# Retention and channel mix in one kernel: blocks 3 to 5 in chunks of 64 tokens, more k buffers, and a new written order

## The chip, the core and the metric

One core of a Trainium2 chip runs the whole program. The metric is the device time of one execution in microseconds (us); lower is better. The figures for the kernel before are three runs and one profiled execution, which the hardware profiler took on that core.

## The reference

Two layers follow each other. The first is a recurrent retention over 768 tokens, for 4 batches and 8 heads of 64:

```
state = gamma[h] * state + outer(k[t], v[t])        # 64 x 64 for each head
y[t]  = 0.125 * q[t] @ state
```

The heads of a token are laid side by side, x (4, 768, 512), and a channel mix follows, in which `x_prev` is x shifted by one token:

```
xk = mu_k * x + (1 - mu_k) * x_prev                 # xr the same with mu_r
out = sigmoid(xr @ w_r) * (relu(xk @ w_k) ** 2 @ w_v)   # w_k 512 x 1024, w_v 1024 x 512, w_r 512 x 512
```

All inputs and the output are float32 in HBM.

## The kernel before

**Blocks.** The 768 tokens of each batch are three blocks of 256, so there are twelve blocks, n = 0 to 11; block n belongs to batch n // 3. The recurrence is computed in chunks: inside a chunk the scores of all pairs of tokens (k against q) are masked to the causal half and multiplied with v, and what came before the chunk enters through a carried state. The products with `w_k`, `w_r` and `w_v` follow for each block; blocks 3 and 4, 6 and 7, and 9 and 10 share one set of mixed inputs (`GROUPS`), so that their key products are 512 tokens wide. All products are in float16 and add up in float32 in PSUM, which has eight banks.

**Three forms of the attention part.** A block takes one of three forms, picked by the lists `HALF` and `WIDE`.

| form | blocks before | chunks | scores (`S`) | masks (`M`) | state updates (`U`) | values (`Y`) and reads of the carried state (`I`, `J`) |
|---|---|---|---|---|---|---|
| in neither list ("plain") | 0, 1 | 2 of 128 | 2 words of 16 products, 64x128 (line 393); block 0 in quarters | two 128x1024; block 0 four 128x512 | 2 | `Y` 32 of 64x128 (line 552) with the second read in it, `I` 8 |
| `WIDE` | 2, 3, 4, 5 | 2 of 128 | 2 words of 8 products, 64x128 (line 385) | two 128x1024 | 2 | `Y` 16 of 128x128 (line 541); `I` 8 and `J` 8 (line 504) |
| `HALF` | 6 to 11 | 4 of 64 | one word of 32 products, 64x64 (line 372) | one 128x1024 | 4 | `Y` 32 of 64x64 (line 525) and 16 of line 504; `I` 16 |

The last block of a batch has one state update fewer, the first block of a batch has fewer reads. In the `HALF` form the result of a block (`D`, line 570) is two VectorE operations of 128x512, in the others one of 128x1024 (line 577).

**Turning q and k.** Both have to stand with the head's 64 elements on the partitions. Blocks 3 to 5 do this with eight full 128x128 products for a head pair each (`PAIRQ`, `PAIRK`, line 308), blocks 6 to 8 with 32 products of 64x64 (line 303), blocks 0 to 2 with 16 of 128x64 (line 314), and blocks 9 to 11 with a DMA transpose on SyncE's queue (`DT`, line 348). ScalarE copies what TensorE turned out of PSUM (line 262).

**Order.** Nothing is scheduled: the string `ORDER` is read word by word, and each word appends its instructions to the engines it uses, so the order of the words is the order on each engine and on each queue. A word is `code.block.part@banks~engine`; `v`, `a`, `p`, `s` are VectorE, ScalarE, GpSimd and SyncE. The codes used below:

| code | what | engine |
|---|---|---|
| `lq`, `lk`, `lv` | loads of a block; POOL's queue except the first half of block 0's q and k, which go through SyncE's queue into a staging tile and are cast by ScalarE (`cq`, `ck`) | DMA |
| `wk.0`, `wk.1`, `wr`, `wv.0`, `wv.1` | loads of weights, POOL's queue | DMA |
| `mu` | four small loads of mu_k and mu_r (line 743); `mt`, `me` turn them and copy them out | DMA |
| `z` | filler products of zeros (lines 758, 765): `z.n` is n//4 in float32 and n%4 in float16 | TensorE |
| `Tq`, `Tk`; `Eq`, `Ek` | turn q, k by TensorE; copy out | TensorE; ScalarE |
| `tq`, `tk` | DMA transposes | SyncE's queue |
| `vs` | v times its decay (line 277) | VectorE |
| `S`, `M` | scores, masks (line 417) | TensorE, VectorE |
| `C`, `U`, `G` | state products; updates (line 482, the first of a batch a copy, lines 262 or 264); decay into the next block | TensorE, VectorE or ScalarE |
| `I`, `Y`, `J` | read of the carried state, values, second read | TensorE |
| `D`, `dx` | the block's result x; its difference to the token before (line 592) | VectorE |
| `X.n.0.j`, `X.n.1.j` | mixed inputs xk, xr of head pair j (line 618) | VectorE |
| `K`, `Qa`, `Qb` | keys (lines 632 and 642), relu, square | TensorE, ScalarE, ScalarE |
| `R`, `s` | gate products (line 672), sigmoid | TensorE, ScalarE |
| `V`, `Vc`, `O`, `st` | values of the channel mix (lines 684, 702), result, store | TensorE, VectorE, SyncE's queue |

**Buffers.** q, k and v stand in rings of four tiles (`RING`), the scaled v and the turned q and k in rings of three, and x in one float32 tile for each of three batches (`xT`, batch b in tile b % (B - 1)). A load into a ring waits for the last reader of the tile that it replaces, and every later load on POOL's queue waits with it.

Of the kernel before, what the change touches and what calls it, by code (L numbers as in the profile page):

```python
# [9 lines left out]
F16 = mybir.dt.float16  # L10
F32 = mybir.dt.float32
# [71 lines left out]
def kernel(  # L83
# [543 lines left out]
    def keys(e, n, g, u=None):  # L627
        t0, t1 = part(u)
        k, m = place[n]
        if joint(n):  # L630
            for co in range(NCO):
                nc.tensor.matmul(  # L632
                    banks("K", n, g), lhsT=wk16[:, co, g * P : g * P + P], rhs=XM[0](k)[:, co, :],
                    start=(co == 0), stop=(co == NCO - 1),
                )
            return
        w = 2 if u is None else 4
        pz = banks("K", n, g, *(() if u is None else (u,))).rearrange("p (i t) -> p i t", i=w)
        for i in range(w):
            fo = w * g + i  # L640
            for co in range(NCO):
                nc.tensor.matmul(  # L642
                    pz[:, i, :], lhsT=wk16[:, co, fo * P : fo * P + P],
                    rhs=XM[0](k)[:, co, m * TM + t0 : m * TM + t1],
                    start=(i == 0 and co == 0), stop=(co == NCO - 1), skip_group_check=True,
                )

# [91 lines left out]
    def load_mu(e):  # L739
        for w, x in enumerate((moe_mu_k, moe_mu_r)):  # L740
            y = x.rearrange("(x r c) -> x r c", x=2, c=D)
            for hp in range(2):
                nc.scalar.dma_start(
                    out=mu8[w * NCO : (w + 1) * NCO, low(hp)], in_=y[:, 1:3] if hp else y[:, 0:4:3]
                )

# [48 lines left out]
    def load_wv(e, h):  # L795
# [8 lines left out]
        "D": yout, "dx": differ, "ax": keep, "X": mixed, "K": keys, "Qa": relued, "Qb": squared, "R": gate,  # L804
# [5 lines left out]
    for word in ORDER.split():  # L810
# [4 lines left out]
        if at:  # L815
# [5 lines left out]
            elif code == "V":  # L821
                key = ("V",) + args[:2]
            BANK[key] = [int(x) for x in at]
        CODES[code](ENG.get(eng), *args)


# [28 lines left out]
```

## Time and profile before

| | |
|---|---|
| three runs | 154.51, 155.25, 155.70 us (median 155.25) |
| the profiled execution | 155.54 us; its span, first to last instruction, 153.7 us, so 1.8 us lie around the span |
| granted TensorE clock | 0.997 |
| busy | TensorE 147.1 us, VectorE 128.1, ScalarE 94.4, GpSimd 62.1 (it issues loads) |
| weight products of 512 columns (lines 684, 672, 632) | 376 |
| weight products of 256 columns (lines 642, 702) | 208 |

A matmul's duration in a listing (380 ns for 512 columns) is longer than the step from one matmul to the next, since they overlap. The chain of waits, which gives each stretch of time once, shows the step: 16 such products in a row take 3.45 us there. In the page, PE is TensorE, PEld its weight loads, DVE VectorE, ACT ScalarE, POOL GpSimd and SP SyncE; an engine with a q behind its name is the engine's queue.

### The profile page before, as it was taken

What the parts mean: (1) busy time and instruction counts of PE and PEld (TensorE: products, weight loads), DVE (VectorE), ACT (ScalarE), POOL (GpSimd) and SP (SyncE); (2) the same over time, 40 slices, a digit from 0 to 9 for tenths busy, and PEclk for the clock granted to TensorE, in tenths of its full rate; (3) what the DMA queues carried; (4) which work ended last, traced back from release to release, by engine and by line L of the source; (5) the groups of instructions that cost most, each with busy time, mean ns of one, the idle gap of its engine ahead of it and who ended that gap; (6) DMA issues with size and microseconds to landing.
All of it is one profiled execution on the core that took longest, in us unless ns stands there. A gap on an engine that the chain in (4) does not pass through costs nothing.

```text
span 153.7 us, 4956 instructions
## 1 busy us (share of the span) xinstructions
PE 147.1 (96%) x2129; PEld 82.7 (54%) x2129; DVE 128.1 (83%) x204; ACT 94.4 (61%) x172; POOL 62.1 (40%) x77
## 2 busy tenths in 40 slices
PE   7799899999999999999999999999999999999991
PEld 3245567657864546445448545446664444466450
DVE  1379999999989999999999996999999999421551
ACT  3474339979864689965518817867541089739430
POOL 7974579977967600499979000000000000000000
PEclk9999999999999999999999999999999999999998
DMA  5999999999999995089999999919103013003153
GB/s 138 264 234 194 182 237 235 157 196 203 194 188 203 249 226 194 11 236 156 255 178 249 219 156 161 183 62 106 35 4 141 0 70 141 0 0 136 68 205 136
DMA packets 56525, 23.83 MB, mean 155 GB/s; under 512 B 48056, under 2 KB 52024, under 8 KB 56504
## 3 DMA queue, kind: packets, MB, share of 16 engines
q0 software_dynamic: 45200, 14.95, 80.5%
q1 hardware_dynamic: 10848, 8.26, 21.9%
q10 hardware_dynamic: 456, 0.32, 0.8%
q8 instruction: 16, 0.26, 0.8%
q14 instruction: 5, 0.04, 0.1%
HBM read 24.31 MB, written 6.29 MB: 199 GB/s over the span
## 4 chain that ended last, share of the span: by engine, by line
PE 70%; DVE 14%; DMA 6%; ACT 4%; issue 2%; ACTq 2%; DVEq 0%
PE ps L684 24%; PE ps L672 12%; PE ps L632 10%; PE ps L642 9%; DMA kT<-k 6%; DVE a L417 3%; DVE xk L618 3%; DVE dx L592 2%; DVE vs L277 2%; PE ps L504 2%; PE ps L765 2%; DVE xT L577 2%; PE ps L308 2%; PE ps L372 1%; PE ps L303 1%
## 5 line engine op out<-in xcount | busy, mean ns | idle before, releaser
L684 PE MATMUL ps<-wv,k2s 128*128 128x512 f16 x184 | 43.9, 380 | 0.2 <-ACT kr L651 0.2
L651 ACT ACTIVATE kr<-ps 128x512 f32<-128x512 f32 x48 | 27.8, 594 | 23.4 <-PE ps L632 14.9
L684 PEld LDWEIGHTS <-k2s 128*128 128x128 f16 x184 | 17.3, 98 | 19.1
L690 DVE SCALAR_TENSOR_TENSOR os<-ps,rs 128x512 f32<-128x512 f32 x23 | 15.1, 683 | 12.9 <-PE ps L684 6.5
L672 PE MATMUL ps<-wr,xr 128*128 128x512 f16 x96 | 24.0, 380 | 0.0
L642 PE MATMUL ps<-xk,wk 128*128 128x256 f16 x192 | 23.6, 273 | 0.1
L256 POOL DMA_DIRECT2D v<-in_v_dram x20 | 18.0, 917 | 13.8 <-DVE vs L277 10.9
L632 PE MATMUL ps<-xk,wk 128*128 128x512 f16 x96 | 22.8, 380 | 0.0
L417 DVE TENSOR_TENSOR a<-ps,c_sb 128x1024 f16<-128x1024 f32 (+1 forms) x20 | 21.8, 1109 | 0.8 <-PE ps L393 0.8
L678 ACT ACTIVATE rs<-ps 128x512 f32<-128x512 f32 x24 | 14.3, 594 | 11.4 <-PE ps L672 8.8
L642 PEld LDWEIGHTS <-wk 128*128 128x128 f16 x192 | 18.1, 98 | 4.4 <-DVE xk L618 0.5
L618 DVE SCALAR_TENSOR_TENSOR xr<-dx,mu,xT 128x256 f16<-128x256 f32 (+1 forms) x36 | 19.3, 564 | 0.0
L618 DVE SCALAR_TENSOR_TENSOR xk<-dx,mu,xT 128x256 f16<-128x256 f32 (+1 forms) x36 | 18.9, 567 | 0.3
L256 POOL DMA_DIRECT2D k<-in_k_dram x20 | 17.8, 916 | 2.6 <-DMA wv<-in_moe_w_v_dram 1.2
L277 DVE TENSOR_TENSOR vs<-v,csm_sb 128x1024 f16<-128x1024 f32 x12 | 14.5, 1214 | 2.7 <-DMA v<-in_v_dram 2.7
L659 ACT ACTIVATE k2s<-kr 128x512 f16<-128x512 f32 x24 | 14.7, 626 | 0.4
L592 DVE TENSOR_TENSOR dx<-xT 128x1024 f32<-128x1024 f32 x12 | 14.6, 1219 | 0.2
L663 ACT ACTIVATE k2s<-kr 128x512 f16<-128x512 f32 x24 | 14.5, 626 | 0.3
L632 PEld LDWEIGHTS <-wk 128*128 128x128 f16 x96 | 9.0, 98 | 10.5 <-issue 0.2
L672 PEld LDWEIGHTS <-xr 128*128 128x128 f16 x96 | 9.0, 98 | 10.0
L262 ACT COPY qT<-ps 128x1024 f16<-128x1024 f16 (+1 forms) x10 | 9.2, 925 | 7.5 <-PE ps L314 3.4
L262 ACT COPY kT<-ps 128x1024 f16<-128x1024 f16 (+1 forms) x10 | 9.3, 934 | 7.1 <-PE ps L303 3.4
(73 smaller groups left out, 153.2 us busy)
## 6 DMA issues: line engine op xcount, KB each, us to landing
out_dram<-os SPq DMA_DIRECT2D x23, 256.0 KB, 3.9
v<-in_v_dram POOLq DMA_DIRECT2D x20, 256.0 KB, 6.3
k<-in_k_dram POOLq DMA_DIRECT2D x21, 128.0 KB, 7.1
q<-in_q_dram POOLq DMA_DIRECT2D x13, 128.0 KB, 7.4
q<-in_q_dram POOLq DMA_DIRECT2D x5, 256.0 KB, 8.1
v<-in_v_dram POOLq DMA_DIRECT2D x2, 512.0 KB, 6.9
wv<-in_moe_w_v_dram POOLq DMA_DIRECT2D x2, 512.0 KB, 7.6
wk<-in_moe_w_k_dram POOLq DMA_DIRECT2D x2, 256.0 KB, 9.6
```

The costliest lines, as they stand in the source:

```text
L256: e.dma_start(out=to[:, i, hs], in_=src[:, i])
L262: e.copy(out=out, in_=in_)
L277: e.tensor_tensor(out=VS(n), in0=V32(n).rearrange("p (h i d) -> p i h d", i=2, h=H), in1=gks[:, int(half(n) or wide(n)), :, :, None].to_br ...
L417: nc.vector.tensor_tensor(out=dst, in0=dst if n in SPLITM else src, in1=mask[:, None, None, :].to_broadcast(list(dst.shape)), op=ALU.mult,)
L592: e.tensor_tensor(out=DX(k)[:, :, m * TM + t0 : m * TM + t1], in0=x[:, :, c + t0 : c + t1], in1=x[:, :, c - 1 + t0 : c - 1 + t1], op=ALU.s ...
L618: nc.vector.scalar_tensor_tensor(out=XM[w](k)[:, j, t0:t1], in0=DX(k)[:, j, t0:t1], scalar=mu[:, w * NCO + j : w * NCO + j + 1], in1=x[:, ...
L632: nc.tensor.matmul(banks("K", n, g), lhsT=wk16[:, co, g * P : g * P + P], rhs=XM[0](k)[:, co, :], start=(co == 0), stop=(co == NCO - 1),)
L642: nc.tensor.matmul(pz[:, i, :], lhsT=wk16[:, co, fo * P : fo * P + P], rhs=XM[0](k)[:, co, m * TM + t0 : m * TM + t1], start=(i == 0 and c ...
L651: nc.scalar.activation(out=kr, in_=banks("K", n, g, *u), func=AF.Relu)
L672: nc.tensor.matmul(banks("R", n, tb), lhsT=XM[1](k)[:, co, t : t + P], rhs=wr16[:, co, :], start=(co == 0), stop=(co == NCO - 1),)
L684: nc.tensor.matmul(banks("V", n, tb), lhsT=K2(n)[:, fo, tb * P : tb * P + P], rhs=wv16[:, fo, :], start=(fo == 0), stop=(fo == NFO - 1),)
L690: nc.vector.scalar_tensor_tensor(out=OS(2 * n + tb), in0=banks("V", n, tb), scalar=1.0 / (KSC * KSC), in1=RS(2 * n + tb), op0=ALU.mult, op ...
```

## The change

Blocks 3, 4 and 5 move from the `WIDE` form to the `HALF` form, still turned by the eight head-pair products. `WIDE` is empty: block 2 becomes plain, its loads included (one DMA in place of two for each of k and v). q and v rings grow from four to five tiles, k's to six, and x has two tiles instead of three. The four loads of mu go through SyncE's queue instead of ScalarE's. A variant of the key products (`keys_by_row`, code `Kp`) is added, which no word of the new order uses.

```diff
-HALF = (6, 7, 8, 9, 10, 11)
+HALF = (3, 4, 5, 6, 7, 8, 9, 10, 11)
-WIDE = (2, 3, 4, 5)
+WIDE = ()
-RING = 4
+RING = 5
+RINGK = 6
+XR = 2
+KP = ()
...
-    K16 = ring("k16_", RING, [H * 2 * D], F16)
+    K16 = ring("k16_", RINGK, [H * 2 * D], F16)
...
-    xT = [const.tile([P, NJ, COLS], F32, name=f"xT{b}") for b in range(B - 1)]
+    xT = [const.tile([P, NJ, COLS], F32, name=f"xT{b}") for b in range(XR)]
...
-        return xT[b % (B - 1)], 1 + bi * TM
+        return xT[b % XR], 1 + bi * TM
...
-                nc.scalar.dma_start(
+                (e or nc.scalar).dma_start(
                     out=mu8[w * NCO : (w + 1) * NCO, low(hp)], in_=y[:, 1:3] if hp else y[:, 0:4:3]
                 )
```

The whole order is written anew. Its beginning and its end, before and after:

```diff
-gy.0 lq.0.0.2~s mu lk.0.0.2~s cq.0.0.2~a lv.0~p z.8@7 Tq.0.0.2@0 ck.0.0.2~a vs.0~v Eq.0.0.2~a
-z.3@1 Tk.0.0.2@1 Ek.0.0.2~a z.3@2 S.0.0.0.2@23 lk.0.2.4~p S.0.1.0.2@45 M.0.1.0.2~v Tk.0.2.4@1
-gy.1~a Ek.0.2.4~a lq.0.2.4~p C.0@67 Tq.0.2.4@0 Eq.0.2.4~a U.0.0~v lv.1~p lk.1~p M.0.0.0.2~v
-U.0.1 z.3@4 S.0.1.2.4@45 M.0.1.2.4~v I.0@01 mt@2 me lq.1~p S.0.0.2.4@67 M.0.0.2.4~v lq.2~p G.0~a
-vs.1~v z.4@3 Y.0 Tk.1@6 Ek.1~a D.0~v dx.0~v z.3@3 Tq.1@7 X.0.0.0 Eq.1~a X.0.1.1 wk.1~p C.1@23
-U.1.0 lk.2~p z.4@4 S.1.1@45 M.1.1~v z.1@0 I.1@01 wk.0~p S.1.0@67 M.1.0~v X.0.0.3 Tq.2@4 Eq.2~a
-z.2@5 Y.1 lv.2~p X.0.0.1 X.0.0.2 z.1@5 K.0.2@4 Tk.2@5 D.1~v X.0.1.0 dx.1~v Qa.0.2 X.0.1.2
-X.1.0.0 Ek.2~a K.0.3@0 Qa.0.3 Qb.0.3 X.1.0.2 X.1.0.1 S.2.1@67 K.0.0@5 Qa.0.0 K.0.1@0 X.1.0.3
-K.1.2@1 K.1.0@5 Qb.0.0 wr~p X.1.1.0 Qa.0.1 U.1.1 G.1~a vs.2~v X.0.1.3 Qa.1.0 Qa.1.2 Qb.0.1
...
+lq.0.0.2~s cq.0.0.2~a lv.0~p lk.0.2.4~p gy.0 z.9@7 Tq.0.0.2@0 lq.0.2.4~p vs.0~v Eq.0.0.2~a
+lv.1~p lk.0.0.2~s ck.0.0.2~a z.5@1 Tk.0.0.2@1 Ek.0.0.2~a z.3@2 S.0.0.0.2@23 M.0.0.0.2~v
+S.0.1.0.2@45 M.0.1.0.2~v Tk.0.2.4@1 Ek.0.2.4~a lq.1~p lk.1~p lk.2~p C.0@67 U.0.0~a Tq.0.2.4@0
+Eq.0.2.4~a lq.2~p U.0.1 z.3@1 S.0.1.2.4@23 lv.2~p mu~s mt@7 G.0~a wk.1~p gy.1~a I.0@45
+M.0.1.2.4~v S.0.0.2.4@01 M.0.0.2.4~v z.4@6 Y.0 me vs.1~v z.5@6 C.1@23 Tk.1@7 Ek.1~a wk.0~p D.0~v
+dx.0~v U.1.0 Tq.1@4 X.0.1.2 z.2@6 Tk.2@5 X.0.0.3 U.1.1 Eq.1~a z.3@6 I.1@01 X.0.0.1 S.1.0@67
+X.0.0.0 X.0.1.0 S.1.1@23 M.1.0~v Tq.2@4 Eq.2~a X.0.0.2 Ek.2~a M.1.1~v z.6@6 Y.1 vs.2~v z.2@6
+K.0.3@2 D.1~v dx.1~v Qa.0.3 G.1~a S.2.1@67 Qb.0.3 lv.3~p K.0.2@0 lk.3~p Qa.0.2 X.0.1.3 C.2@2
+X.0.1.1 X.1.0.2 U.2.0 X.1.0.3 lq.3~p X.1.0.1 S.2.0@45 K.0.0@1 K.0.1@0 Qa.0.0 wr~p I.2@23 X.1.0.0
+K.1.2@1 Qb.0.0 M.2.1~v Qa.0.1 M.2.0~v Qa.1.2 Qb.1.2 vs.3~v K.1.0@0 Qa.1.0 Qb.0.1 lq.4~p Tk.3@1
+Ek.3~a X.1.1.3 lk.4~p Y.2 D.2~v Tq.3@0 Eq.3~a K.1.1@4 K.1.3@5 dx.2~v X.2.0.1 X.2.0.0 X.2.1.3
+C.3@67 Qa.1.1 Qb.1.1 lv.4~p X.2.0.2 S.3@23 U.3.0~a wv.0~p R.0.1@4 s.0.1 R.0.0@0 X.2.0.3 X.1.1.1
+Tq.4@4 s.0.0 Eq.4~a lq.5~p K.2.2@1 Qa.2.2 X.1.1.0 Tk.4@0 Ek.4~a X.1.1.2 R.1.1@4 s.1.1 U.3.1
...
 [after, TensorE's words from K.5.3 to R.10.1, other engines left out]
+K.5.3@6 Tq.8@23 I.7@45 Tk.8@01 K.5.0@6 R.5.0@7 C.8@01 Y.7 R.5.1@2 K.5.1@7 V.4.0.0@6 V.4.0.1
+V.5.0.0@7 V.5.1.0@3 V.5.1.1 S.8@45 I.8@01 V.5.0.1 K.6.1@2 K.6.0@3 K.6.3@2 K.6.2@3 K.6.7@7 C.9@23
+Y.8 C.10@45 K.6.5@7 K.6.6@6 R.7.1@7 R.7.0@0 K.6.4@7 V.7.1.0@6 K.8.2@0 K.8.0@7 S.9@23 I.9@01
+V.7.1.1 K.8.3@7 K.8.1@4 S.10@23 I.10@67 Y.9 V.7.0.0@5 V.7.0.1 V.6.0.0@2 R.6.0@3 S.11@01 Y.10
+C.11@45 V.8.1.0@3 V.8.1.1 V.8.0.0@6 R.6.1@7 V.6.1.0@0 V.6.1.1 V.8.0.1 V.6.0.1 K.9.4@7 K.9.1@0
+K.9.7@1 K.9.3@0 K.9.0@1 I.11@45 K.9.2@7 K.9.6@2 K.9.5@7 Y.11 R.10.0@2 R.9.1@1 R.10.1@7
...
-R.11.1@0 V.11.0.0@7 R.11.0@4 O.9.0 st.9.0 V.11.0.1 O.10.1 s.11.1 st.10.1 s.11.0 O.10.0 st.10.0
-O.11.0 st.11.0 Vc.11.1.0@4 Oc.11.1.0 sc.11.1.0~s Vc.11.1.1@6 Oc.11.1.1 sc.11.1.1~a
+st.10.1 Qb.11.3 Qa.11.2 Qb.11.2 s.11.1 V.11.0.0@2 V.11.0.1 Vc.11.1.0@3 O.11.0 st.11.0 Oc.11.1.0
+sc.11.1.0~s Vc.11.1.1@0 Oc.11.1.1 sc.11.1.1~a
```

On POOL's queue the loads of v, k and q of blocks 0 to 2 now all stand ahead of `wk.1` and `wk.0`; before, `k` of block 2 stood between the two and `v` of block 2 behind both. Later on that queue, `lv.11` now stands ahead of `lv.7` and 21 further loads. On SyncE's queue the DMA transposes now follow as `tq.9`, `tk.9`, `tk.11`, `tq.10`, `tk.10`, `tq.11`.

More of the change, by code (lines that the diff above doesn't have):

```diff
@@ new lines @@
+X.2.1.2 G.3~a U.4.0 U.4.1 Qb.2.1 wv.1~p U.4.2 Qa.2.3 U.4.3 lv.6~p X.2.1.0 V.0.0.0@2 lk.5~p
+R.1.0@3 s.1.0 I.4@45 X.2.1.1 lv.5~p Y.3 R.2.1@1 V.0.1.0@3 Qb.2.3 Qb.0.2 D.3~v Tq.5@6 Y.4 Qb.2.2
+Qb.1.0 V.1.1.0@7 lk.6~p V.0.1.1 V.1.1.1 dx.3~v D.4~v dx.4~v X.3.0.3 X.3.0.0 lq.6~p R.2.0@4
+Tk.5@5 X.3.0.1 X.3.0.2 Qa.2.0 O.0.1 st.0.1 V.1.0.0@0 V.1.0.1 O.1.0 Qb.2.0 V.0.0.1 O.0.0 O.1.1
+vs.5~v lk.7~p X.3.1.0 K.3.3@3 V.2.1.0@0 vs.6~v Ek.5~a G.4~a s.2.1 lq.7~p Eq.5~a Qa.3.3 V.2.1.1
+Tk.6@67 st.1.0 s.2.0 Qb.3.3 Ek.6~a lv.11~p S.5@23 Tq.6@45 M.5~v lv.7~p K.3.6@1 Eq.6~a Qa.3.6
@@ new lines @@
+X.3.1.1 K.3.7@6 S.6@45 Qa.3.7 Tk.7@23 Ek.7~a K.3.5@1 O.2.1 lv.8~p M.6~v Tq.7@67 Qa.3.5 lk.9~p
+Eq.7~a C.5@23 U.5.0 st.0.0 lq.9~p U.5.1 K.3.0@0 K.3.2@1 Qa.3.0 Qb.3.6 Qa.3.2 U.5.2 I.5@45
+X.3.1.2 C.6@67 U.6.0~a X.3.1.3 U.6.1 U.6.2 S.7@23 M.7~v U.6.3 vs.7~v K.3.1@0 V.2.0.0@1 K.3.4@6
+I.6@23 Qb.3.0 Qa.3.1 Y.5 D.5~v R.4.1@7 dx.5~v X.5.1.2 X.5.1.0 X.5.0.2 st.2.1 R.3.0@0 Qb.3.1
+s.4.1 Qb.3.2 V.2.0.1 O.2.0 X.5.0.0 st.2.0 Qa.3.4 Qb.3.4 X.5.0.3 Qb.3.5 R.3.1@4 s.3.1 X.5.1.3
+R.4.0@6 Qb.3.7 V.3.0.0@7 st.1.1 Y.6 s.3.0 C.7@45 V.4.1.0@0 vs.8~v s.4.0 G.6~a U.7.0 lq.8~p
@@ new lines @@
+X.5.0.1 U.7.1 V.3.0.1 D.6~v V.4.1.1 tq.9~s O.4.1 U.7.2 U.7.3 K.5.2@6 Qa.5.2 G.7~a V.3.1.0@1
+V.3.1.1 O.3.1 K.5.3@6 lv.9~p X.5.1.1 Qa.5.3 Tq.8@23 I.7@45 lk.8~p Tk.8@01 Ek.8~a Qb.5.2 Eq.8~a
+K.5.0@6 O.3.0 st.3.1 R.5.0@7 C.8@01 Y.7 R.5.1@2 s.5.0 K.5.1@7 Qa.5.0 Qb.5.0 V.4.0.0@6 dx.6~v
+Qb.5.3 vs.9~v st.3.0 U.8.0 U.8.1 Qa.5.1 D.7~v dx.7~v X.6.0.1 X.6.0.0 X.6.1.0 U.8.2 Qb.5.1
+V.4.0.1 V.5.0.0@7 X.6.0.2 V.5.1.0@3 V.5.1.1 S.8@45 I.8@01 X.6.0.3 V.5.0.1 s.5.1 O.5.1 K.6.1@2
+Qa.6.1 K.6.0@3 O.4.0 lv.10~p lq.10~p Qa.6.0 Qb.6.0 O.5.0 K.6.3@2 Qa.6.3 lk.10~p st.5.0 K.6.2@3
@@ new lines @@
+Qa.6.2 X.6.1.3 Qb.6.3 K.6.7@7 C.9@23 vs.10~v Qa.6.7 M.8~v Y.8 Qb.6.7 C.10@45 st.5.1 K.6.5@7
+tk.9~s st.4.1 X.6.1.2 lq.11~p Qb.6.2 K.6.6@6 X.6.1.1 Qa.6.5 R.7.1@7 Qb.6.1 U.9.0~v D.8~v dx.8~v
+X.8.0.2 X.8.0.0 X.8.0.1 s.7.1 X.8.0.3 Qa.6.6 Qb.6.6 R.7.0@0 s.7.0 K.6.4@7 Qa.6.4 V.7.1.0@6
+Qb.6.5 lk.11~p tk.11~s K.8.2@0 Qb.6.4 U.9.1 U.9.2 K.8.0@7 U.9.3 S.9@23 G.9~v Qa.8.2 Qa.8.0
+I.9@01 X.8.1.2 tq.10~s U.10.0 V.7.1.1 K.8.3@7 Qb.8.0 Qa.8.3 U.10.1 M.9~v U.10.2 U.10.3 K.8.1@4
+G.10~a O.7.1 tk.10~s Qa.8.1 S.10@23 Qb.8.1 vs.11~v tq.11~s I.10@67 Y.9 M.10~v V.7.0.0@5 D.9~v
@@ new lines @@
+R.8.0@4 X.11.1.1 R.9.0@0 R.8.1@5 X.11.1.3 X.11.0.3 s.9.1 V.10.1.0@1 s.8.0 s.8.1 Qb.9.6 Qb.9.4
+V.9.1.0@5 V.10.0.0@4 V.10.0.1 s.9.0 V.9.0.0@0 V.9.0.1 X.11.0.0 O.8.0 R.11.0@6 O.8.1 s.10.1
+st.8.1 st.8.0 X.11.0.1 K.11.3@7 s.10.0 Qa.11.3 K.11.1@2 Qa.11.1 Qb.11.1 K.11.0@7 Qa.11.0 Qb.11.0
+K.11.2@2 V.10.1.1 V.9.1.1 st.7.1 O.10.0 st.10.0 O.9.0 s.11.0 st.9.0 R.11.1@0 O.9.1 st.9.1 O.10.1
+st.10.1 Qb.11.3 Qa.11.2 Qb.11.2 s.11.1 V.11.0.0@2 V.11.0.1 Vc.11.1.0@3 O.11.0 st.11.0 Oc.11.1.0
+sc.11.1.0~s Vc.11.1.1@0 Oc.11.1.1 sc.11.1.1~a
@@ L644, in keys, with keys_by_row @@
                     rhs=XM[0](k)[:, co, m * TM + t0 : m * TM + t1],
+                    start=(i == 0 and co == 0), stop=(co == NCO - 1), skip_group_check=True,
+                )
+    def keys_by_row(e, n, gp, co):
+        k, m = place[n]
+        for g in (2 * gp, 2 * gp + 1):
+            pz = banks("K", n, g).rearrange("p (i t) -> p i t", i=2)
+            for i in range(2):
+                fo = 2 * g + i
+                nc.tensor.matmul(
+                    pz[:, i, :], lhsT=wk16[:, co, fo * P : fo * P + P],
+                    rhs=XM[0](k)[:, co, m * TM : m * TM + TM],
                     start=(i == 0 and co == 0), stop=(co == NCO - 1), skip_group_check=True,
@@ L803 @@
         "S": scores, "N": moved, "M": masked, "C": state, "U": summed, "G": decayed, "I": inter_off, "Y": intra, "J": inter_on,
-        "D": yout, "dx": differ, "ax": keep, "X": mixed, "K": keys, "Qa": relued, "Qb": squared, "R": gate,
+        "D": yout, "dx": differ, "ax": keep, "X": mixed, "K": keys, "Kp": keys_by_row, "Qa": relued, "Qb": squared, "R": gate,
         "s": opened, "V": values, "O": result, "st": store, "gy": powers, "wk": load_wk,
@@ L823 @@
             BANK[key] = [int(x) for x in at]
+            if code == "Kp":
+                for g in range(2):
+                    BANK["K", args[0], 2 * args[1] + g] = [int(at[g])]
         CODES[code](ENG.get(eng), *args)
```

46 lines of the change are left out of this document (7 added, 39 removed).

## The prediction

> **What bounds the kernel now.** I read the slices of the page first, then the groups, the timeline of the first 40 us engine by engine, the chain of waits, and the waits.
>
> ```profile
> PE   7799899999999999999999999999999999999991
> DVE  1379999999989999999999996999999999421551
> ...
> PE 70%; DVE 14%; DMA 6%; ACT 4%; issue 2%; ACTq 2%; DVEq 0%
> ```
>
> TensorE is full from the eighth slice on, and VectorE nearly as full until the last six. The chain tells which of them sets the time: TensorE after some 28 us, VectorE before. So the end is: when the ramp hands over to TensorE, plus the products that are left, plus the little that TensorE then stands idle. How large a product is, the chain shows by its steps:
>
> ```profile
> 76.13 3.45 PE ps L684 x16
> 136.65 1.75 PE ps L642 x16
> 63.28 0.86 PE ps L632 x4
> 80.11 0.97 PE ps L672 x4
> 65.39 0.26 PE ps L429 x32
> 71.43 0.38 PE ps L429 x32
> 37.42 0.55 PE ps L385 x16
> 60.40 0.38 PE ps L372 x32
> 32.10 0.57 PE ps L541 x16
> 109.66 0.38 PE ps L525 x32
> 35.19 0.37 PE ps L447 x16
> 47.66 0.24 PE ps L504 x8
> 79.58 0.26 PE ps L504 x16
> 50.85 0.45 PE ps L308 x8
> ```
>
> A word of four 512-column products takes 0.86 us, of eight 256-column ones 0.87. The third and fourth row, and the fifth and sixth, are equal work; the longer one follows products of another shape. A change of shape costs 0.11 us.
>
> **Part 1: three blocks in the other form.** Take each word where it follows a weight product. Scores: 0.55 (WIDE) against 0.38 (HALF). Values: 0.57 against 0.38. State products: 0.37 against 0.38. Reads of the carried state: two words of 8 (0.24 each) against two of 16 (0.26 each). Together 1.97 against 1.66: 0.3 less for a block, 0.9 for three. Turning stays at 0.45 a word. Block 2 as a plain block I take at -0.1: its products are of line 393's and 552's kind, which stand in the ramp and hide behind VectorE there; bounds are 0 and -0.3. From the first key product on I count 56 changes of shape in the old order and 48 in the new, 0.9 us less. Some 1.9 us of TensorE's time go.
>
> A page of the Trainium skill speaks against this. "TensorE: Matmul & The Clock Gate", in Part 1, says that matmuls never start closer than about 25 ns, however few columns they have; by it 32 products of 64 columns take 0.8 us, scores, values, reads and state of three blocks would gain some 4 us instead of losing 0.9, and the end would be near 158. The trace disagrees: 32 products of line 372 take 0.38, 12 ns each. With that row there I give it no chance.
>
> On VectorE three masks go and six updates come, and the three results are two operations each:
>
> ```profile
> 18.12 2.35 DVE L417 TENSOR_TENSOR a<-ps,c_sb 128x1024 f16<-128x1024 f32 x2
> 88.61 1.33 DVE L482 TENSOR_TENSOR tg<-ps,tg 128x256 f16<-128x256 f32 x3
> 74.22 1.47 DVE L570 TENSOR_TENSOR xT<-ps,gy_sb 128x512 f32<-128x512 f32 x2
> 14.40 1.22 DVE L577 TENSOR_TENSOR xT<-ps,gy_sb 128x1024 f32<-128x1024 f32 x1
> ```
>
> That is -3 x 1.17 + 6 x 0.44 + 3 x 0.25 = -0.1 us; one update and one decay less on VectorE make it -1. It lies beside TensorE's products after 28 us and counts as nothing there; without that cover it would be 1 us the other way, a gain.
>
> **Part 2: the ramp.** Here the order decides, so I follow it to one point, the first key product of block 2 (K.2.0 before, K.2.2 after).
>
> ```profile
> 1.05 3.78 PE L758 MATMUL ps<-zero 128*128 128x512 f32 x4 [1.05 <-DVE xT L737]
> 3.63 1.27 ACTq L743 DMA_DIRECT2D mu<-in_moe_mu_r_dram  x2
> 4.94 0.62 ACT L262 CAST q<-k2s 128x512 f16<-128x512 f32 x1 [1.81 <-DMA k2s<-in_q_dram]
> 5.61 0.64 PE L314 MATMUL ps<-c_sb,q 128*64 128x128 f16 x8 [0.78 <-ACT q L262]
> 6.18 1.46 PE L765 MATMUL ps<-zero 128*128 128x512 f16 x3
> 7.94 1.23 DVE L277 TENSOR_TENSOR vs<-v,csm_sb 128x1024 f16<-128x1024 f32 x1 [2.69 <-DMA v<-in_v_dram]
> 9.53 0.42 PE L393 MATMUL ps<-qT,kT 64*64 64x128 f16 x16
> 10.95 0.82 PE L765 MATMUL ps<-zero 128*128 128x512 f16 x3
> ...
> k2s<-in_q_dram SPq DMA_DIRECT2D x1, 256.0 KB, 3.3
> ```
>
> With mu on SyncE's queue ScalarE's queue is free by 3.1, and q, issued at 0.74, lands at 4.0: the cast starts 0.9 us earlier. That alone gains little, because the filler z.9 holds TensorE until about 5.2. What decides is when TensorE turns fast: three fillers take 1.46 us at 6.18 and 0.82 at 10.95. Before, TensorE stood still from 4.8 to 5.6 and was fast some 3.9 us after it started again. In the new order nothing interrupts it from 1.05 on. Bounds: fast from 5.0 (1.05 + 3.9), or as before from 9.5. If fast by 7, k is turned at 7.1 (its cast now follows the copy of q), the scores stand at 8.5, and then v's landing binds: decay done at 9.2, two masks, an update, two masks (the second pair waits for the copy of q's second half, which now stands behind an update on ScalarE), the next decay, and block 0's result D.0 starts at 13.4. If slow until 9.5, the larger filler z.5 delays the scores to 9.85 and D.0 to 15.05. Before it was 14.40. I take 13.6, near the early bound, since no gap is left in which TensorE could lose its speed.
>
> The skill's rule for this, "TensorE: Matmul & The Clock Gate", Part 1, is a free-running window of about 3.4 us that has to be busy as a whole. By it the new order is fast between 4.5 and 7.9, and D.0 between 13.4 and 14.2.
>
> ```profile
> 21.43 1.09 PE L642 MATMUL ps<-xk,wk 128*128 128x256 f16 x8
> 24.82 1.66 DVE L618 SCALAR_TENSOR_TENSOR xk<-dx,mu,xT 128x256 f16<-128x256 f32 x4
> 29.39 2.34 DVE L417 TENSOR_TENSOR a<-ps,c_sb 128x1024 f16<-128x1024 f32 x2
> 37.91 1.05 PE L642 MATMUL ps<-xk,wk 128*128 128x256 f16 x8
> 150.56 0.42 DVE L709 SCALAR_TENSOR_TENSOR os<-ps,rs 128x256 f32<-128x256 f32 x1 [0.45 <-PE ps L702]
> ```
>
> From D.0 VectorE runs without a gap. Between D.0 and the end of block 2's masks the old order has two results and two differences (1.2 each), 14 mixes (0.41), three updates (0.38), four masks and a decay (1.15): 17.3 us, and 14.40 + 17.3 = 31.7, which is the end of the third row. The new order has 12 mixes there: 16.5. So the masks end at 30.1, 1.6 earlier. TensorE starts its keys later, at 22.5 against 21.43: its first key word now stands behind Y.1, which waits for the mask M.1.1 at 21.5. K.1.2 waits for its mixes until 27.8, Y.2 for the masks until 30.1, and K.2.2 for block 2's mixes until 13.6 + 22.5 = 36.1, 1.8 us ahead of K.2.0's 37.9. But then two gate words that the old order had done are still to do (1.73).
>
> The loads would have to be late to undo this:
>
> ```profile
> DMA packets 13373, 6.19 MB, mean 206 GB/s; under 512 B 10170, under 2 KB 12858, under 8 KB 13370
> ```
>
> Up to and with wk.0 the new queue holds 4.6 MB, 22.5 us at that rate; K.0.0 needs wk.0 at about 25, so 2 us are left. Before, K.0.0 ran at 24.5.
>
> **Part 3: the sum.** From that first key product to the last product the old order holds 93.5 us of weight products, and 17.2 of small ones by the prices above: 110.7. The trace took 112.6 (37.9 to 150.5), so 1.9 us are idle. The new order holds 95.2 and 16.4: 111.6. With the same 1.9 it ends at 36.1 + 111.6 + 1.9 = 149.6, 0.9 before the old one. The tail (VectorE's last result, the store) is the same. The profiled execution took 155.54; less 0.9 that is 154.6. It lay 0.3 over the median of the three runs, so for a median I forecast 155.25 - 0.9, rounded to **154.3 us**.
>
> **Part 4: taken as nothing.** Larger rings only let loads start earlier; TensorE hides them, and before they cost at most what is in the first row here. Two x tiles instead of three: batch 2's first result D.6 overwrites batch 0's, whose last reader, a mix of block 2, was done 30 us earlier; if not, D.6 would wait on its own engine. The transposes follow st.5.1 at about 91 with all loads landed; S.9 needs the first ones at 103.
>
> ```profile
> POOL v L256 <- DVE vs L277: 10.9, 1, 10.9
> PE ps L372 <- DMA kT<-k: 0.4, 1, 0.4
> ```
>
> The wait of POOL's queue moves: lv.11 now waits for vs.6 at about 58, and lv.7 and 21 loads wait behind it. v of block 7 is due on VectorE at 67; before, the loads behind that wait landed within 9 us. No cost, up to 1 us if they take as long as the slowest of the ramp.
>
> **The rivals.**
> *No idle is left* (152.4, chance 0.2). Part of the 1.9 us are waits that the new order takes away: block 10's scores for a transpose that ran among loads (second row above), block 8's keys for VectorE's mixes. Then 1.9 us less. Against it: the ends of bank uses stand close everywhere.
> *TensorE turns fast as late as before* (155.7, chance 0.15). D.0 at 15.05, and all of Part 2 1.45 later. For it: only one start is in the trace. Against: the gap is gone.
> *Slower: ScalarE hands banks back late* (157.1, chance 0.17). Between K.5.0 and V.9.1.0 I count 22 places where a product needs a bank that ScalarE empties at most 0.4 us earlier by my sums: bank 7 serves K.6.7, K.6.5, R.7.1, K.6.4, K.8.0, K.8.3 in turn.
>
> ```profile
> L651 ACT ACTIVATE kr<-ps 128x512 f32<-128x512 f32 x48 | 27.8, 594 | 23.4 <-PE ps L632 14.9
> L659 ACT ACTIVATE k2s<-kr 128x512 f16<-128x512 f32 x24 | 14.7, 626 | 0.4
> ```
>
> A relu and a square together take 1.2 us against 0.86 for a key word, so where a square stands between two relus the margin is gone. Before, five places share the 1.9 us, 0.38 each. With 12 of 22 at 0.38 the idle is 4.6: 147.7 + 4.6 = 152.3, 1.8 later than before. From seven such places on it isn't faster any more. Against: ScalarE has 23.4 us of idle ahead of its relus.
>
> **How the numbers follow.** Forecast 0.48, the rivals 0.2, 0.15 and 0.17. The forecast's own range is 153.4 to 155.2 (D.0 at 13.4 to 14.2, idle 1 to 2.5). Range: 152.0 (D.0 at its early bound, no idle) to 157.0 (the slower rival). About 1% is what a measurement here tells from no change, so faster is under 153.7 and slower over 156.8: faster 0.2 and three tenths of the forecast's 0.48, 0.34; slower 0.17 and a rest of the late start, 0.20; within 0.46.
>
> **What would show it.** Right: fillers of 0.22 us each ahead of the first scores, D.0 near 13.6, the first key product near 22.5, block 2's near 36, TensorE's last product near 149.6, line 372 at 12 ns a product in blocks 3 to 5. Wrong: D.0 after 14.4; waits of TensorE for ScalarE's relus in the windows from 80 to 130 us; VectorE standing at vs.7 near 67 us; or a first key product of block 2 after 37 us.

## The result and the profile after

Twenty runs of each kernel, taken in turn on the same chips, gave a median of 155.81 us for the changed kernel (155.09 to 157.79) and 154.81 us for the one before (153.65 to 156.69). The ratio is 1.0079, with a 95% interval of 1.0054 to 1.0104: slower by 0.8%, where 0.9 us less was forecast. The ratios, here and below, leave out runs in a slower state, so they are not the quotients of the medians. The profiled execution of the changed kernel took 157.79 us with a granted clock of 0.989, and is the longest of its twenty: in three of them the clock fell like this, in the other seventeen it is 0.996 or more. A second profile, without the fall, is used beside it (first experiment).

From the page of the changed kernel, the slices and the shares of the chain:

```profile
PE   7979989999999999999985999999999999999991
DVE  1479999999999999989957799998999992983051
...
PEclk9999999999999999999998799999999999999999
...
PE 53%; DVE 25%; DMA 14%; issue 4%; POOL 1%; SPq 0%; DVEq 0%; POOLq 0%
```

Before, TensorE had no slice under 9 between the fifth and the last. Now the 21st and 22nd are 8 and 5, and VectorE has a dip beside them. The granted clock falls in the 22nd and 23rd. DMA has 14% of the chain against 6%.

The ramp first, from the timelines of TensorE and VectorE: fillers, the results of blocks 0 to 2, block 2's first key product, TensorE's last word.

```profile
4.63 0.63 PE L781 MATMUL ps<-zero 128*128 128x512 f16 x1
5.76 1.27 PE L774 MATMUL ps<-zero 128*128 128x512 f32 x2
6.87 0.38 PE L781 MATMUL ps<-zero 128*128 128x512 f16 x1
14.28 1.22 DVE L580 TENSOR_TENSOR xT<-ps,gy_sb 128x1024 f32<-128x1024 f32 x1
36.50 1.04 PE L645 MATMUL ps<-xk,wk 128*128 128x256 f16 x8
150.90 1.91 PE L718 MATMUL ps<-wv,k2s 128*128 128x256 f16 x16
```

One filler takes 0.63 at 4.63 and 0.38 at 6.87: fast by then, as forecast. Block 2's first key product starts at 36.50 (forecast 36.1). From there to the end of the last product it is 116.3 us, and the forecast was 113.5, 1.9 of it idle. More than these 2.8 us are lost in one place (2.06 us of standing and some 1.7 of a slow clock, below), and part of the forecast's idle didn't come. The place, in the timelines of VectorE and TensorE:

```profile
79.98 0.43 DVE L485 TENSOR_TENSOR t<-ps,tg 128x256 f32<-128x256 f32 x1
82.80 0.69 DVE L706 SCALAR_TENSOR_TENSOR os<-ps,rs 128x512 f32<-128x512 f32 x1 [2.39 <-DMA out_dram<-os]
81.27 0.21 PE L306 MATMUL ps<-c_sb,k 64*64 64x64 f16 x2
83.55 0.44 PE L306 MATMUL ps<-c_sb,k 64*64 64x64 f16 x30 [2.06 <-DVE os L706]
```

And in the chain of waits, in order of time:

```profile
74.34 0.33 SPq L713
74.67 0.05 issue
74.72 7.98 DMA out_dram<-os
...
82.80 0.70 DVE os L706
...
83.55 0.44 PE ps L306 x30
```

VectorE's 82.80 is the word O.3.1, a result. It writes one of four result tiles (`OS`, tile 7 % 4 = 3), and the tile still holds O.1.1, made at about 56. The store of O.1.1, st.1.1, stood ahead of st.2.1 and st.2.0 in the old order and stands behind both in the new one. SyncE's queue issues in order, so st.1.1 waited for O.2.0's end at 74.3, and then landed 8 us after its issue, among loads and the first transpose. O.3.1 stood 2.39 us for it; it empties bank 1, in which half of Tk.8 (block 8's k turned) is to be written, so TensorE stood 2.06 us in the middle of that word. In the kernel before, st.1.1 was issued at 56.7 us, and the same result (there from line 690, with O.3.0 behind it) has no wait:

```profile
79.06 1.28 DVE L690 SCALAR_TENSOR_TENSOR os<-ps,rs 128x512 f32<-128x512 f32 x2
```

What followed in the changed kernel shows in the windows (columns: stretch, its length, busy time of PE, PEld, DVE, ACT, POOL, then granted clock, DMA share, GB/s):

```profile
82.00:84.00 2.00, 0.46 (x31) 0.41 (x31) 1.20 (x3) 0.00 (x0) 0.87 (x1) 1.00 1.23 114
84.00:86.00 2.00, 2.00 (x11) 1.22 (x12) 2.00 (x3) 1.97 (x3) 0.00 (x0) 0.65 2.49 151
86.00:88.00 2.00, 2.00 (x75) 1.14 (x72) 1.18 (x2) 1.56 (x3) 0.00 (x0) 0.50 2.19 197
```

After the stand TensorE worked on, at 0.65 and then 0.50 of its clock in these two windows: that is 1.7 us of full-speed work less.

### The profile page after: what moved, and what is told of

It is laid out like the page before. It is cut to its first block, busy times and chain, and to the rows that moved or that the text cites. A ratio compares the mean times of both kernels' runs of the same rounds, so it can differ in the third digit from the quotient of the medians.

```text
span 156.0 us, 5432 instructions
## 1 busy us (share of the span) xinstructions
PE 147.6 (95%) x2367; PEld 83.7 (54%) x2367; DVE 127.4 (82%) x207; ACT 95.4 (61%) x180; POOL 60.3 (39%) x75
## 4 chain that ended last, share of the span: by engine, by line
PE 53%; DVE 25%; DMA 14%; issue 4%; POOL 1%; SPq 0%; DVEq 0%; POOLq 0%
PE ps L700 16%; PE ps L688 9%; PE ps L635 9%; DMA v<-in_v_dram 9%; PE ps L645 7%; DMA out_dram<-os 5%; DVE vs L280 5%; DVE xk L621 4%; DVE a L420 3%; DVE dx L595 3%; DVE xr L621 3%; DVE os L706 2%; DVE xT L573 2%; PE ps L507 2%; DVE xT L580 2%
## 5 line engine op out<-in xcount | busy, mean ns | idle before, releaser
L667 ACT ACTIVATE kr<-ps 128x512 f32<-128x512 f32 x48 | 28.5, 596 | 23.9 <-PE ps L635 12.2
L700 PE MATMUL ps<-wv,k2s 128*128 128x512 f16 x184 | 43.0, 379 | 0.0
L259 POOL DMA_DIRECT2D v<-in_v_dram x18 | 16.2, 923 | 12.1 <-DVE vs L280 9.5
L420 DVE TENSOR_TENSOR a<-ps,c_sb 128x1024 f16<-128x1024 f32 (+1 forms) x17 | 18.3, 1091 | 0.6 <-PE ps L396 0.4
L259 POOL DMA_DIRECT2D k<-in_k_dram x18 | 15.9, 893 | 3.6 <-ACT k2s L679 1.4
L573 DVE TENSOR_TENSOR xT<-ps,gy_sb 128x512 f32<-128x512 f32 x18 | 12.4, 689 | 4.2 <-PE ps L507 3.0
```

What stands on the lines that cost most here:

```text
L259: e.dma_start(out=to[:, i, hs], in_=src[:, i])
L420: nc.vector.tensor_tensor(out=dst, in0=dst if n in SPLITM else src, in1=mask[:, None, None, :].to_broadcast(list(dst.shape)), op=ALU.mult,)
L573: nc.vector.tensor_tensor(out=x[:, :, :, v], in0=banks("I", n)[:, v].rearrange("p (j i t) -> p j i t", j=NJ, i=2), in1=g[:, :, :, v], op=A ...
L667: nc.scalar.activation(out=kr, in_=banks("K", n, g, *u), func=AF.Relu)
L700: nc.tensor.matmul(banks("V", n, tb), lhsT=K2(n)[:, fo, tb * P : tb * P + P], rhs=wv16[:, fo, :], start=(fo == 0), stop=(fo == NFO - 1),)
```

## The experiments

Theory A: the store behind the others is the loss. Theory B: the loads that wait behind lv.11 on GpSimd's queue (9.45 us of wait, up to 59.5; called the pause below) come as a burst and are the loss. Rivals from the prediction: the ramp, and the form of blocks 3 to 5. Ratios are to the kernel before, run in turn on the same chip. Every edit is against the changed kernel unless it says otherwise.

**e0_after_again.** No edit: a second profile.

> The new kernel once more, for a second profile. If the first profile's 2.3 us ahead of Tk.8 is in every execution, it is here too, within 0.7 us, with st.1.1 issued near 74 us and landing near 82. If the drop of the clock to 0.5 behind it is what makes the first profile longer than most runs (157.8 against a median of 155.8), it is missing here, the span is near 154.0, and block 2's first key product is near 36.5 again. If the wait is a matter of chance, it is missing here.

155.44 us (two runs), ratio 1.0043 [0.9966, 1.0121]; the profiled run 155.43, clock 1.0.

```profile
81.76 0.69 DVE L706 SCALAR_TENSOR_TENSOR os<-ps,rs 128x512 f32<-128x512 f32 x1 [1.41 <-DMA out_dram<-os]
82.50 0.44 PE L306 MATMUL ps<-c_sb,k 64*64 64x64 f16 x30 [1.07 <-DVE os L706]
```

The stand is there, 1.07 us, and the clock isn't touched. So the wait is in both profiles, and the fall of the clock does not come with it each time.

**e1_store and e1_again.** Only the store moves.

```diff
-Tk.6@67 st.1.0 s.2.0
+Tk.6@67 st.1.0 st.1.1 s.2.0
...
-V.3.0.0@7 st.1.1 Y.6
+V.3.0.0@7 Y.6
```

> One word moved in the new order: st.1.1 stands right behind st.1.0 instead of behind st.2.0 on SyncE's queue. Theory A (the result O.3.1 waits for the store st.1.1, which stands too late on the queue; bank 1, and so Tk.8, waits with it): O.3.1 has no wait for a store, TensorE's 2.3 us ahead of Tk.8 near 81 us are under 0.4, the clock stays at 1.00 in all slices, the span is 152.0 to 152.8 and the time 0.5 to 1.5 us under the kernel before. Theory B (the loads that GpSimd issues in one burst behind lv.11 are the cause, whatever waits for them): VectorE then waits at the next place that needs a transfer, and the end moves by under 1 us. Theory C (the chunks of 64 cost TensorE more than my prices): the wait may go, but the end stays within 0.5 us of the new kernel's.

> The changed kernel with st.1.1 right behind st.1.0, once more, on the chip of the three others. If the first result holds: median 153.5 to 154.4, ratio to the kernel before 0.988 to 0.995. If it was the chip's luck: 1.000 to 1.008 as the changed kernel.

153.94 us, ratio 0.9916 [0.9884, 0.9948]; on another chip 154.39, ratio 0.997 [0.9938, 1.0002]. The second median is just inside what was expected if the first result holds, and the second ratio lies between the two expectations: the gain is clear against the changed kernel (1.0079), but smaller than the first time. TensorE's waits from 75 to 85 us in the first of the two:

```profile
76.67 0.93 PE L645 MATMUL ps<-xk,wk 128*128 128x256 f16 x7 [0.23 <-DVE xk L621]
81.30 1.03 PE L645 MATMUL ps<-xk,wk 128*128 128x256 f16 x8 [0.32 <-ACT kr L667]
```

Nothing is left of the stand in Tk.8. In e1_again TensorE stood another 0.49 us in the middle of Y.5 at 67.7 (more on such stands under e3_both), and VectorE waited 1.39 us for v of block 7.

**e6_tile.** The store stays where the change put it; O.3.1 gets a result tile of its own.

```diff
-    OS = ring("os_", 4, [dm], F32)
+    OS5 = ring("os_", 5, [dm], F32)
+    OS = lambda i: OS5(4 if i == 7 else i % 4)
```

> The changed kernel, with a fifth result tile that only O.3.1 uses; the store st.1.1 stays where it was, behind st.2.0. Theory A (O.3.1 stood because its tile was still being stored): O.3.1 has no wait for a store, block 8's keys (Tk.8) take at most 0.8 us, TensorE's last product ends at 149 to 150.5, median 153.8 to 154.8, at most 1.000 of the kernel before. Theory B (the late store crowds the DMA engines and delays other work too): Tk.8 is short but the end gains less than half of what moving the store gained, median 154.9 to 155.5.

154.06 us, ratio 0.9964 [0.9931, 0.9997]; TensorE ends at 149.6.

```profile
80.18 0.42 DVE L486 TENSOR_TENSOR t<-ps,tg 128x256 f32<-128x256 f32 x1
80.52 0.68 DVE L707 SCALAR_TENSOR_TENSOR os<-ps,rs 128x512 f32<-128x512 f32 x1
```

O.3.1 follows the update without a wait, though st.1.1 is as late as in the changed kernel. So the loss is the reuse of the tile, and not the traffic of the late store. Theory A is shown by two edits that have only this in common.

**e2_load, e3_both.** lv.11 moves from ahead of lv.7 to ahead of lq.11; in e3_both the store moves too.

```diff
-Ek.6~a lv.11~p S.5@23
+Ek.6~a S.5@23
...
-tk.9~s st.4.1 X.6.1.2 lq.11~p
+tk.9~s st.4.1 X.6.1.2 lv.11~p lq.11~p
```

> One word moved in the new order: lv.11 stands in front of lq.11, so that lv.7 and the other loads do not wait for vs.6. The store st.1.1 stays where it is. Theory A (position of the store): st.1.1 is still issued near 74 us; O.3.1, due near 80.4, still waits 1 us or more if a store beside the transpose tq.9 lands in more than 7 us; the gain is under 1 us. Theory B (the burst of loads crowds the store): the loads run from 50 us on and are over by 78, vs.7 does not wait (0.7 before), the store lands in 3 to 4 us instead of 8, O.3.1 does not wait, and the gain is that of the run with the store moved, 1.5 to 3.5 us against the new kernel. Theory C: no change of the end.

> Both words moved (st.1.1 early, lv.11 late). Theory A and B agree that no wait of VectorE over 0.5 us is left between 55 and 90 us, and that the time is 153.2 to 153.9 where the kernel before has 154.8: 1.4 us under it, since block 2's first key product stands at 36.5 and 111.9 us of products and 0.6 of idle are left. Theory C: not under the kernel before.

156.83 us, ratio 1.011 [1.0065, 1.0156], and 157.16, ratio 1.0137 [1.0079, 1.0196]. Theory B falls: without the pause the kernel is no faster with the late store (1.011 against 1.0079, intervals that overlap), and 3.2 us slower with the early one (e3_both against e1_store, same chip). TensorE in e3_both, and the DMA queues for the four early stores, e1_store first (window 54 to 58) and e3_both second (same window):

```profile
61.41 0.29 PE L432 MATMUL ps<-vs,k 64*64 64x64 f16 x12
63.81 0.31 PE L432 MATMUL ps<-vs,k 64*64 64x64 f16 x12 [2.12 <-issue]
```

```profile
out_dram<-os SPq DMA_DIRECT2D x4, 256.0 KB, 2.4
```

```profile
out_dram<-os SPq DMA_DIRECT2D x4, 256.0 KB, 7.5
```

Each of the four stores lands in 2.4 us in the pause and in 7.5 without it (medians). TensorE stands 2.12 us in the middle of C.5, between two products of the same word, and no semaphore is named ("issue"). Among the DMA packets are pieces of 16 KB on a queue called instruction, about every 6 us, and the piece due then is late. Window 58 to 59 in e1_store, and 61 to 62 in e3_both (columns: packets, MB, share of the 16 DMA engines):

```profile
q8 instruction: 1, 0.02, 6.1%
```

```profile
q8 instruction: 1, 0.02, 6.0%
```

Between 58 and 61 e3_both has none. In the eight profiles of the new order with the pause and the full rings, that piece starts at 58.2 to 59.0 and C.5 doesn't stand; in e2_load and e3_both it starts at 61.7 and 61.6, ends 1 us later, and TensorE goes on at 64.0 and 63.8. All seven stands of 0.15 us and more for which the profiles name no releaser (these two, 0.81 in e3_both, 0.49 in e1_again, 0.16 in e4_filler, 0.84 and 0.85 in e5_form) end 1.2 to 1.5 us after the end of such a piece. So it seems that the program's own instructions queue with the loads, and that TensorE ran out of them. That is read from their times; no run moved such a piece alone. The Trainium skill ("Runtime: NRT & Kernel Launch", Instruction fetch mechanics) says that an engine's instructions are refilled over DMA in blocks of 16 KiB, and that this is mostly hidden: the blocks are here in that size, but with the DMA engines full it wasn't hidden. 2.1 to 2.6 us are this stand, and in e3_both another 0.81 of the same kind follows in Y.5. In e2_load the stand also covers most of the later one: O.3.1 still waited 1.08 us for its store, and TensorE, late by then, had no wait for it. That would explain why the two kernels without the pause differ little from each other, and the two with it by 1.1 to 1.6% (1.0079 against 0.997 and 0.9916).

**e4_filler.** Fillers (z.10: two in float32, two in float16) ahead of Tk.8, so that TensorE stays busy in the stand.

```diff
-Tk.8@01
+z.10@0 Tk.8@01
```

> The new order with filler products of zeros (z.10, bank 0) right in front of Tk.8, where TensorE stands for 2.3 us; the wait itself stays. If the drop of the granted clock to 0.5 near 86 us comes from that stand (theory: idle TensorE loses its clock), it does not come with the filler: the clock is 1.00 in all slices, no run of this kernel is over 156.5, and its median is 0.3 to 1 us under the new kernel's. If the drop comes of its own, or if the filler holds Tk.8 up, the time is the same or up to 0.5 us longer.

156.12 us, ratio 1.0095 [1.0062, 1.0128]: no better than the changed kernel. O.3.1 still waited 1.38 us for the store, the fillers took 2.35, and the clock was 1.0. Its twelve runs all have a clock of 0.997 or more, against three falls in the changed kernel's twenty; that is too few to show that the fillers keep the clock up. Three of the twelve are over 156.5 at full clock, which the theory had ruled out. The fillers are longer than the stand: O.3.1 was done at 82.28, and Tk.8 started behind them at 83.54. So they cost some 1.2 us in every run, where a fall of the clock costs some 1.7 in three of twenty.

**e5_form.** The kernel before, with only the form of blocks 3 to 5 changed. Their words are joined or split as the form asks, and nine of them (I, Y, D, C of blocks 3 to 5 and Tq.7) moved a few places to suit, and C.5 took other banks; other places might do better.

```diff
-HALF = (6, 7, 8, 9, 10, 11)
-WIDE = (2, 3, 4, 5)
+HALF = (3, 4, 5, 6, 7, 8, 9, 10, 11)
+WIDE = (2,)
```

> The kernel before, with only the form of blocks 3 to 5 changed to chunks of 64 (block 2 stays WIDE, rings and loads as before; the words that the form no longer has are left out, C.5 takes banks 2 and 3, and reads, values and two products around them are moved apart so that TensorE's writes to a bank stay in order). My price (0.3 us a block less on TensorE, and 9 changes of shape at 0.11 less at most): TensorE's products between K.2.0 and the end take 1 to 1.9 us less, the time is 0.5 to 1.5 us under the kernel before, if the moved words cost no waits. Theory C (the form costs TensorE more than that): the same time or longer, with line 372, 525 and 429 of blocks 3 to 5 dearer than in blocks 6 to 8.

161.49 us, ratio 1.0384 [1.0317, 1.045]. Four of TensorE's waits:

```profile
40.16 1.92 PE L637 MATMUL ps<-xk,wk 128*128 128x256 f16 x16 [0.88 <-DVE tg L477]
45.12 0.32 PE L499 MATMUL ps<-qT,tg 64*64 64x64 f16 x14 [0.77 <-DVE tg L477]
47.68 0.28 PE L499 MATMUL ps<-qT,tg 64*64 64x64 f16 x9 [0.84 <-issue]
87.63 0.19 PE L520 MATMUL ps<-a,vs 64*64 64x64 f16 x1 [0.85 <-issue]
```

All of them from 40 us on add up to 5.1 us, against 0.5 before. The chunks of 64 form a chain: a chunk's read of the state waits for VectorE's update of the chunk ahead, and in the old order too few products stand between. The second row is such a wait, and a third one for tg (0.30, at 44.13) too. In the first row it is a key word (K.2.3 on bank 6) that waits until the updates of block 3 have read that bank, four of them where there were two. The three are 2.0 of the 5.1; two stands with no releaser are 1.7. Nor are the products any shorter: from block 2's first key product (37.77) to the end (155.08) it is 117.3 us, less 5.1 of waits 112.2, against 112.6 less 0.5, or 112.1, before. So the saving that was priced for the form isn't seen here, and the form needs an order made for it.

**e7_rings.** Four tiles for q, k and v in the new order.

```diff
-RING = 5
-RINGK = 6
+RING = 4
+RINGK = 4
```

> The new order with all rings of four tiles as before (RING = RINGK = 4, x still in two tiles). Theory of the prediction (larger rings count as nothing, TensorE hides the loads): within 0.5 us of the new kernel. Rival (the new order leans on the larger rings: lq.4, lk.4 and lv.4 stand where block 0's tiles are just free, and lk.5 to lv.8 early): GpSimd's queue waits, the loads come late, and it is 1 us or more slower than the new kernel.

161.85 us, ratio 1.0465 [1.0399, 1.0532].

```profile
68.44 0.27 PE L432 MATMUL ps<-vs,k 64*64 64x64 f16 x4 [7.09 <-DMA k<-in_k_dram]
```

C.5 stands 7.09 us for a k: lk.9 stands ahead of it and, with four tiles, fills the tile of block 5, so C.5 reads block 9's k and has to wait for it. So this kernel no longer computes the same thing, and its time is no price of a smaller ring by itself. It shows that the order is written for the larger rings.

**e8_gap.** e1_store, with a gap in TensorE's first 5 us.

```diff
-gy.0 z.9@7 Tq.0.0.2@0
+gy.0 z.4@7 Tq.0.0.2@0
```

> The changed kernel with the early store (st.1.1 right behind st.1.0) and the first filler cut from z.9 to z.4, so that TensorE stands still from about 2.9 to 4.5 us. Theory (an uninterrupted start is what makes TensorE fast early, and the ramp sets the end): the products turn fast only at about 8.5, the first scores start at 9.2 to 9.9 instead of 8.5, D.0 starts at 14.2 to 14.9 instead of 13.5, and the median is 154.4 to 155.3 against 153.9. Rival 1 (fast time depends on the time since the start, not on the gap): D.0 at 13.5 or earlier, median 153.3 to 153.9. Rival 2 (the ramp's delay is taken up later): D.0 late, median within 0.3 of 153.9.

154.72 us against 154.39 of e1_again on the same chip; ratio 1.0005 [0.9971, 1.004].

```profile
4.55 0.64 PE L317 MATMUL ps<-c_sb,q 128*64 128x128 f16 x8 [1.42 <-ACT q L265]
6.98 0.63 PE L781 MATMUL ps<-zero 128*128 128x512 f16 x1
7.55 0.64 PE L317 MATMUL ps<-c_sb,k 128*64 128x128 f16 x8
8.12 0.83 PE L781 MATMUL ps<-zero 128*128 128x512 f16 x3
13.83 1.22 DVE L580 TENSOR_TENSOR xT<-ps,gy_sb 128x1024 f32<-128x1024 f32 x1
```

With the gap the products are slow until 8.1, some 1.5 us longer than in e1_again. But D.0 is only 0.35 late (13.83 against 13.48 in e1_again), not the 0.7 to 1.4 I expected: without the long filler q is turned 0.6 us earlier, and that would give half of it back. The 0.33 us of the medians agree with the 0.35, though the intervals are wider than that.

**e9_lv7.** e1_store with one load ahead of the pause instead of behind it.

```diff
-Ek.6~a lv.11~p S.5@23 Tq.6@45 M.5~v lv.7~p K.3.6@1
+Ek.6~a lv.7~p lv.11~p S.5@23 Tq.6@45 M.5~v K.3.6@1
```

> The changed kernel with the early store, and lv.7 moved ahead of lv.11 on POOL's queue; the pause of that queue until vs.6 stays. Theory (vs.7 waits for v only because lv.7 stands behind the pause): vs.7's wait of 0.7 us is gone, VectorE runs up to 0.7 us earlier from 67 us on, TensorE's waits of 0.2 for mixes near 76 us go, the early stores still land within 3 us and no word stands in its middle; median 153.3 to 153.9. Rival (the pause has to stay clear of loads): the stores or the instruction loads near 58 us get slower, TensorE stands in mid-word near 62 us, median 154.5 to 156.

153.28 us, ratio 0.9903 [0.987, 0.9937], against 154.39 of e1_again on the same chip. VectorE at vs.7, e1_store first, then e9_lv7:

```profile
67.78 1.23 DVE L280 TENSOR_TENSOR vs<-v,csm_sb 128x1024 f16<-128x1024 f32 x1 [0.74 <-DMA v<-in_v_dram]
```

```profile
66.77 0.41 DVE L485 TENSOR_TENSOR t<-ps,tg 128x256 f32<-128x256 f32 x1
67.10 1.22 DVE L280 TENSOR_TENSOR vs<-v,csm_sb 128x1024 f16<-128x1024 f32 x1
```

The wait is gone, and TensorE's 0.23 and 0.32 near 76 and 81 us with it: after 20 us TensorE has one wait of over 0.15 us left, 0.16. Its ratio is the lowest of all, 1% under the kernel before.

## Why the prediction was wrong

**The step that failed is Part 4, "taken as nothing".** It asked whether larger rings, two x tiles, the transposes and GpSimd's wait cost anything, and did not look at the stores: a store that holds its tile longer stood in the sum at nothing. The order moved st.1.1 past two other stores on SyncE's queue, and with that it moved the end of a result tile's use: the "ring of four" that mattered was `OS`, which the diff doesn't touch. Its price: O.3.1 waited 1.41 and 2.39 us and TensorE 1.07 and 2.06 in two profiles; between the medians' ratios of e6_tile and of the changed kernel lie 1.15%, 1.8 us. Part 4 also placed all the transposes behind st.5.1, with all loads landed; the first, tq.9, stands right behind st.1.1 and was issued at 75.3, among the loads and beside that store. How much of the store's 8 us is due to it, no run shows.

**"No cost, up to 1 us" for lv.11 was mis-sized.** The sign that I named as wrong, VectorE standing at vs.7 near 67 us, did come: 0.66 us in the changed kernel, 0.74 and 1.39 in e1_store and e1_again. Putting lv.7 ahead of the pause gave 1.1 us on one chip, just beyond the upper bound; part of it is the 0.49 that e1_again stood in Y.5. The pause itself, which I took for a risk, was worth 3.2 us (e3_both against e1_store).

**Part 2, the ramp, held.** Fast by 6.9, D.0 at 14.28 in the first profile, just beyond the 14.2 of the forecast's own range, where TensorE waited 0.60 for a load of k and 0.35 for the scaled v, and at 13.46 to 13.81 in e0_after_again, e1_store, e1_again and e9_lv7 (forecast 13.6). Block 2's first key product came at 35.65 to 36.50 in the profiles of the new order with full rings (36.1). The rule of the Trainium skill that the prediction weighed here ("TensorE: Matmul & The Clock Gate", Part 1: a free-running window of about 3.4 us) put the turn between 4.5 and 7.9, and the first trace agrees: slow at 4.63, fast at 6.87. In e2_load and e4_filler fillers at 4.30 and 4.46 already take 0.38, a little earlier than a window that is busy as a whole allows.

**Part 3, the sum, held in its total for a kernel without the store's wait.** Forecast for the end of TensorE: 149.6. Measured: 148.6 (e1_store), 149.6 (e6_tile), 148.3 (e9_lv7). From e9_lv7's 35.83 to 148.28 it is 112.45 us with 0.16 of waits, so the products take 112.3 instead of 111.6, and the idle of 1.9, taken over from the old order, is nearly nothing: two errors of 0.7 and 1.7 that partly cancel, which is luck. The 1.9 was a misreading already: in the trace of the kernel before, TensorE's waits of 0.15 us and more after 37.9 add up to 0.5 (0.16 and 0.35), so most of the 1.9 was product time that the prices had missed, and neither rival that works with 1.9 of idle had so much to take or to share out. By their ratios e1_store, e1_again and e6_tile lie 0.8, 0.3 and 0.4% under the kernel before; the forecast was 0.6%.

**Part 1.** 32 products of 64x64 take 0.38 and less in blocks 3 to 5 too; Y.4 and S.5 in the chain of waits of e9_lv7:

```profile
47.02 0.38 PE ps L528 x32
57.11 0.27 PE ps L375 x32
```

12 and 8 ns each, so what the Trainium skill states there ("TensorE: Matmul & The Clock Gate", Part 1: starts never closer than about 25 ns) does not hold for these. But e5_form shows what Part 1 left out: the form brings waits of its own, over 4 us where the order doesn't make room for them. The 0.9 us that Part 1 priced for three blocks, and the changes of shape beside it, were not found there (112.2 against 112.1 us of products); why not, stays open.

**The rivals.** ScalarE late with its banks: one wait of 0.32 in e1_store, none in e9_lv7. TensorE fast as late as before: no. No idle left (152.4): e9_lv7 comes near it with 153.28, by an edit that the change did not make.

## What to carry to other kernels

When an order is rewritten, follow each buffer's last reader and not only its next writer: a store that slips behind another on an in-order queue holds its tile, and the price appears 25 us later on an engine that has nothing to do with stores. A pause in the loads can be useful: here stores landed in it in 2.4 us instead of 7.5, and a piece of the program's own instructions came 3 us earlier. Before filling such a pause, look at what lands in it. Move the one load that is needed soon to the front, and leave the pause.

## What the hardware showed that I had not expected

- TensorE can stand in the middle of a word, it seems for its own instructions: 2.12 and 2.57 us where the 16 KB piece came 3 us late, in a stretch in which stores of 256 KB took 7.5 us instead of 2.4 (e3_both against e1_store). All seven stands without a named releaser end 1.2 to 1.5 us after the end of a 16 KB piece.
- In the profiles a stand of 2.06 us (changed kernel) and one of 2.57 (e2_load) were followed by a granted clock of 0.50, 1.1 and 1.4 us after their ends; one of 2.12 (e3_both) and one of 1.07 were not. The clock fell under 0.99 in 3 of 20 runs of the changed kernel, in 4 of 6 of e2_load and in 4 of 6 of e3_both, and in none of e1_store, e1_again, e6_tile and e9_lv7 (46 runs). The length of the stand alone doesn't decide.
- What may decide is the place of the stand on a beat. By the profiles' record of the granted clock, its changes lie whole multiples of 3.413 us apart: at 6.09, 84.60 and 88.02 us in the changed kernel (23 and 1 of them), at 3.97, 65.41 and 68.83 in e2_load (18 and 1). On that beat, the changed kernel stood 2.06 us of the beat ahead of the fall, and e2_load 1.99. In e3_both, whose first change is at 4.76, a beat ends at 62.8 and cuts the stand of 2.12 (61.70 to 63.81) into 1.09 and 1.02. So it fits these profiles that the idle time within one beat counts, with a limit between 1.1 and 2.0 us; no run moved a stand on the beat.
- A start with a gap of 1.4 us turned fast at about 8.1, 3.6 us after the gap. Without a gap it turned fast between about 4.0 (e2_load) and 6.9, 2.9 to 5.8 us after the first product.
